# Value tables of a linear-attention kernel: loaded one tile earlier, split in steps, four differences on POOL

## The chip, the cores and the metric

One core of a Trainium2 chip. The metric is the device time of one launch in microseconds, the median of several runs. Times inside a run are microseconds from the start of the profiled span. The engines are PE (TensorE), DVE (VectorE), ACT (ScalarE), POOL (GpSimd) and SP, whose queue issues most transfers.

## The reference

The input x is 2048 tokens by 640 columns. It is normalised and goes into an attention branch and an MLP branch, whose product is added to x. Only the attention's value projection is touched here.

```python
xn = _layernorm(x, axis=-1)
qkv = (xn @ wqkv)                       # 32 heads of 20
pq = einsum("bhsd,hdf->bhsf", q, w_phi) # the same for k
phi = concat([softmax(pq), softmax(-pq)], axis=-1)
kv = einsum("bhsf,bhsd->bhfd", phi_k, v); z = sum_s(phi_k)
o = (phi_q @ kv) / (phi_q @ z + 1e-6)
return x + (o @ wo) * silu(gelu(xn @ w1 + b1) @ w2 + b2)
```

## The kernel before

Tokens are cut into 16 tiles of 128 rows; two tiles make a token pair (`q`). Matmuls work on values split into a high part, rounded to the fp32r format, and a low part, the difference to the original: three passes (high by high, high by low, low by high) make one product. So each weight table is read as a raw fp32 row buffer, copied by ACT into the high part of a slab (`AF.Copy`), and the low part is a subtraction on DVE or POOL.

The first phase runs its code in the order written: every engine carries out its instructions in that order, and a wait holds up all that is behind it on the engine. SP's queue is in that order as well.

*Tiles 6 to 9* (loop `for t in range(6, 10)`): per tile a key projection (`project`, L372), its feature, a value projection and two query projections. `feat1` makes a feature's exponents: three DVE instructions (maximum L384, subtraction L387, minimum L390), one on POOL (L391); `feat2` is ACT's exponential (L400), and `store_e` writes a query's feature to memory through ACT's queue (L695). In the same loop the transposed input of a later token pair is normalised: `pair_sub` on POOL (L341), `pair_mul` on DVE (L346), `pair_plain` rounds it (ACT L285, DVE L287), `t_sums` forms sums of blocks on POOL (L300) and `t_split` rounds those (ACT L321, POOL L323). `pair_stats` stores a pair's mean and deviation (L332) and reads them back spread over the partitions (L334).

*Tiles 10 to 15* (loop `for p in range(5, 8)`): two key projections, then `kv_pair` (L452), which adds the two tiles before to the key-value state and needs POOL's scaled key features (L413), then a value pair. A value pair computes the values of two tiles by a scheme of seven matmul groups (`QPARTS`, L663), which I name X, Y, X2, V, Z, W and S4 in their order. They use sums and differences of weight blocks, made earlier and kept in memory (`sv_dram`, four tables of 128 x 640). Y and V use the first two tables (slabs named `ws`), Z and W the halves that replace part of the direct value weights (`wv`), S4 a slab of two further halves (`ws` again). After X and Y ACT copies the banks to `qx` (L667, L669); V waits for the second copy, X2 for the first. POOL adds the two copies to `qu` (L670), DVE adds V (L674) and then Z (L677), which S4 waits for.

The four tables are loaded at tile 9 (`forms`, L155) and split by `split_to` (L608, L609): the first two after tile 9's last query feature, the `wv` halves between the two key projections of tile 10, the S4 halves inside the value pair, their copies after X and Y (L628), their differences after W (L632), all differences on DVE. The dumps of two query tables (`w_dump`, L208) and the transposed input of pair 7 (`load_xr`, L266, L267) follow the loads on SP.

Row buffers and slabs come from rotating pools; a buffer is taken again when its last reader or its store is done.

Of the kernel before, what the change touches and what calls it, by code (L numbers as in the profile page):

```python
# [8 lines left out]
F32 = mybir.dt.float32  # L9
F32R = mybir.dt.float32r  # L10
AF = mybir.ActivationFunctionType
OP = mybir.AluOpType
# [9 lines left out]
HALF = D // 2  # L22
# [24 lines left out]
def hedgehog_gated_mlp_kernel(ctx: ExitStack, tc: tile.TileContext, x, xt_in, wqk, bd, wv, wo, w1, b1, w2, b2, out_t):  # L47
    nc = tc.nc
# [4 lines left out]
    dram = ctx.enter_context(tc.tile_pool(name="dram", bufs=1, space=bass.MemoryType.DRAM))  # L53
# [27 lines left out]
    def slab(dt, name, shape=(P, 2, D)):  # L81
        return slabs.tile(list(shape), dt, tag="S", name=name)

    def row(shape, dt, name):
        return rows.tile(shape, dt, tag="R", name=name)
# [13 lines left out]
    sv_dram = dram.tile([4, P, D], F32, name="sv_dram")  # L99
# [52 lines left out]
    def load_raw(src, blk=None):  # L152
        raw = row([P, D], F32, "raw")
        dst = raw[:] if blk is None else raw[:].rearrange("p (a b) -> p a b", b=blk)
        nc.sync.dma_start(dst, src)  # L155
        return raw
# [50 lines left out]
    def w_dump(c):  # L207
        nc.sync.dma_start(wq_dram[c], wq_s[c][:, :, :HALF].bitcast(F32))  # L208
# [53 lines left out]
    def load_xr(q):  # L262
        h, p = divmod(q, SLOTS)
        xr = slab(F32, "xr", (P, KC, W2))[:]
        src = xt_in.rearrange("(k p) (h o q t) -> p k h o q t", p=P, h=NH, o=2, q=SLOTS)[:, :, h, :, p]
        nc.sync.dma_start(xr[:, :, :P], src[:, :, 0])  # L266
        nc.sync.dma_start(xr[:, :, P:], src[:, :, 1])  # L267
        xrs[q] = xr
# [25 lines left out]
    def spill(q):  # L294
        nc.sync.dma_start(xp_dram[:, :8, :, at(q)], xp[:, :, :, at(q)].bitcast(F32))
        nc.sync.dma_start(xp_dram[:, 8:, :, at(q)], beside(q).bitcast(F32))
# [47 lines left out]
    def pair_mul(q):  # L344
        bc, xr = pld.pop(q), xrs[q]
        nc.vector.tensor_tensor(xr, xr, bc[:, None, :, 1].to_broadcast([P, KC, W2]), op=OP.mult)  # L346
# [16 lines left out]
    def project(t, ws, mid=None, at_k=3):  # L363
        q, o = divmod(t, 2)
        ps = bankA()
        n = 0
        for k in range(KC):
            if k == at_k and mid is not None:
                mid()
            for a, b in PASSES:  # L370
                for hf in range(2):
                    nc.tensor.matmul(ps[:, hf, :HALF], stat_x(q, o, k, a),  # L372
                                     ws[k][:, b, hf * HALF:(hf + 1) * HALF],
                                     start=n == 0, stop=n == 3 * KC - 1)
                n += 1
        return ps

    def heads(ps):
        return ps[:, :, :HALF].rearrange("p a (h d) -> p a h d", d=DH)

    def feat1(ps, later=None):
        p4 = heads(ps)
        mx = small.tile([P, 2, 16], F32, tag="mx", name="mx")
        nc.vector.tensor_reduce(mx[:], p4, axis=AX.X, op=OP.max)  # L384
        e = slab(F32, "e")[:]
        e5 = e.rearrange("p a (h s d) -> p a h s d", s=2, d=DH)
        nc.vector.tensor_tensor(e5[:, :, :, 0, :], p4, mx[:, :, :, None].to_broadcast([P, 2, 16, DH]),  # L387
                                op=OP.subtract)
        nr = small.tile([P, 2, 16], F32, tag="nr", name="nr")
        last_feat[0] = nc.vector.tensor_reduce(nr[:], e5[:, :, :, 0, :], axis=AX.X, op=OP.min)  # L390
        rest = lambda: nc.gpsimd.tensor_tensor(e5[:, :, :, 1, :], nr[:, :, :, None].to_broadcast([P, 2, 16, DH]),  # L391
                                               e5[:, :, :, 0, :], op=OP.subtract)
        if later is None:
            rest()
        else:
            later.append(rest)
        return e.rearrange("p a b -> p (a b)")

    def feat2(ef):
        nc.scalar.activation(ef, ef, AF.Exp)  # L400
        return ef
# [56 lines left out]
    def kv_pair(t):  # L458
        for u in (t, t + 1):
            kv_acc(u, phis.pop(u), vs.pop(u))  # L460
# [70 lines left out]
    wv_s = []  # L531
# [72 lines left out]
        wq_b.append(sl)  # L604
        nc.sync.dma_start(sl[:, :, :HALF].bitcast(F32), wq_dram[c])

    def split_to(dst, src, eng):
        nc.scalar.activation(dst[:, 0], src, AF.Copy)  # L608
        eng.tensor_tensor(dst[:, 1], src, dst[:, 0].bitcast(F32), op=OP.subtract)  # L609

    def forms(dram, f, base, engs, s4_last=False):
        raws = [load_raw(dram[k]) for k in range(4)]
        yield
        for k in range(4):
            if k < 3:
                f.append(slab(F32R, "ws"))
            if k < 2:
                split_to(f[k][:], raws[k][:], engs[k])
            else:
                split_to(base[k - 2][:, :, HALF:], raws[k][:, HALF:], engs[k])  # L620
            if k == 2 and s4_last:
                continue
            parts = [(f[2][:, :, (j - 2) * HALF:(j - 1) * HALF], raws[j][:, :HALF], engs[j])
                     for j in ((2, 3) if s4_last and k == 3 else (k,) if k >= 2 else ())]
            if s4_last and k == 3:
                yield
            for d, r, _ in parts:
                nc.scalar.activation(d[:, 0], r, AF.Copy)  # L628
            if s4_last and k == 3:
                yield  # L630
            for d, r, eng in parts:
                eng.tensor_tensor(d[:, 1], r, d[:, 0].bitcast(F32), op=OP.subtract)  # L632
            yield

    QPARTS = (("X", "A11", 0, None), ("Y", "S2", 10, None), ("X", "A12", 2, ("A1k", 4)), ("V", "S3", 12, ("A2k", 7)),
# [68 lines left out]
    wq_f, wq_b, wv_f = [], [], []  # L704
# [6 lines left out]
    for t in range(6, 10):  # L711
        q = t - 3
        pk = project(t, wk_s)
        if t == 8:
            kv_pair(6)
            spill(3)
        if t == 9:
            vb = forms(sv_dram, wv_f, wv_s, [nc.vector] * 4, True)
            next(vb)
            w_dump(0)  # L720
            w_dump(1)
        if t == 6:
            next(vf[1])
        es[t] = feat1(pk)
        if t > 6:
            feat2(es[t])
            pair_mul(q)
            pair_plain(q)
            t_sums(q)
        else:  # L730
            pair_sub(4)
            fold_w(wqT, range(4, KC), "wq", wq_s)
            feat2(es[t])
        vs[t] = value(t)
        phis[t] = key_fin(es.pop(t))
        pq = project(next(queries), wq_s)
        ef = feat1(pq)
        if t > 6:
            t_split(q)
            load_xr(q + 1)  # L740
        for u in STATS.get(t, ()):
            pair_stats(u)
        store_e(queries_done.pop(0), ef)
        pq = project(next(queries), wq_s)
        ef = feat1(pq)
        if t == 6:
            next(vf[1])
        if t == 9:
            next(vb)
            next(vb)  # L750
        if t in (7, 8):
            pair_sub(q + 1)
        store_e(queries_done.pop(0), ef)
        if t == 6:
            kv_pair(4)
        for u in XIN.get(t, ()):
            x_in(u)
    qf, later, last_sums = None, [], []
    for p in range(5, 8):
        t = 2 * p  # L760
        pk = project(t, wk_s)
        if p == 7:
            w1r = load_w1(0)
            qf = forms(sq_dram, wq_f, wq_b, [nc.vector, nc.vector, nc.vector, nc.gpsimd])
            next(qf)
        es[t] = feat1(pk)
        if p == 5:
            next(vb)
        if p == 6:
            pair_plain(7)  # L770
        pk = project(t + 1, wk_s)
        kv_pair(t - 2)
        es[t + 1] = feat1(pk, later)
        if p == 7:
            next(qf)
            next(qf)
            q_back(0)
            q_back(1)
            wq_b.extend(wq_s[2:])

        def rest(t=t, p=p):
            if p == 5:
                next(vb)
            later.pop(0)()
            feat2(es[t])
            if p == 6:
                t_sums(7)
            if p == 7:
                next(qf)

        def first_key(t=t, p=p):
            if p == 5:
                next(vb)
            phis[t] = key_fin(es.pop(t))
            feat2(es[t + 1])

        def second_key(t=t, p=p):
            if p < 7:
                phis[t + 1] = key_fin(es.pop(t + 1))
            else:  # L800
                phis[t + 1] = es.pop(t + 1)
                last_sums.append(key_sums(phis[t + 1]))
            if p == 5:
                pair_mul(7)
            if p == 6:
                t_split(7)

        value_pair(p, {1: rest, 2: lambda: p == 7 and next(qf), 3: lambda: p == 5 and pair_sub(7), 4: first_key, 6: second_key})
# [525 lines left out]
```

## Time and profile before

| what | value |
|---|---|
| time, median of 3 runs (657.24 to 657.57) | 657.42 us |
| the profiled execution's own time | 660.41 us |
| its span | 658.7 us |
| mean granted TensorE clock | 0.995 |
| instructions in the span | 11422 |

The profile's page gives each engine's busy time, the slices of the span, and the costliest groups. Other views: the list of waits of one engine (who was waited for, total, times, longest); the timeline (start, duration, engine, line, operation, what it writes and reads, count, and in brackets the idle time before it with its releaser); windows (start and end, length, busy time with count, clock, DMA share, rate).

### The profile page before, as it was taken

To read this page: it belongs to the slowest core of one execution; us is meant where nothing else is said; L and a number is where in the kernel's file an instruction comes from. 1 tells how busy PE (TensorE), PEld (TensorE's weight loads), DVE (VectorE), ACT (ScalarE), POOL (GpSimd) and SP (SyncE) were. 2 spreads that over 40 slices of the span, in tenths; PEclk is the share of its full clock that TensorE was granted. 3 is DMA by queue.
4 is the path that set the end of the run, shared out by engine and by line. 5 is a ranking of instruction groups with operands and counts; after the bars stand their busy time and mean duration, and the time that the engine had idled before them with its cause. 6 is when DMAs were issued, how large, how long until landed. Compare 5 with 4: busy or idle time off the path is not lost.

```text
span 658.7 us, 11422 instructions
## 1 busy us (share of the span) xinstructions
PE 649.6 (99%) x4396; PEld 563.9 (86%) x4396; DVE 488.3 (74%) x739; ACT 237.6 (36%) x345; POOL 396.8 (60%) x366
## 2 busy tenths in 40 slices
PE   9999999999799999999999999999999999999997
PEld 9999999999799998888888888888888886766866
DVE  5785976788976778768979968759789899853232
ACT  3512323324333246252452454751332424132130
POOL 2755477897767864857778876363462967343321
PEclk9999999999799999999999999999999999999999
DMA  9705286466311387537899799596779399999942
GB/s 351 273 1 176 83 295 199 129 212 213 120 42 41 99 270 256 176 102 258 229 256 313 180 410 318 105 331 237 156 215 251 79 266 199 310 244 241 330 162 80
DMA packets 164447, 135.15 MB, mean 205 GB/s; under 512 B 89394, under 2 KB 128562, under 8 KB 164010
## 3 DMA queue, kind: packets, MB, share of 16 engines
q1 hardware_dynamic: 161658, 122.84, 63.7%
q10 hardware_dynamic: 2736, 11.60, 4.5%
q8 instruction: 34, 0.56, 0.4%
q14 instruction: 19, 0.16, 0.1%
HBM read 86.03 MB, written 48.38 MB: 204 GB/s over the span
## 4 chain that ended last, share of the span: by engine, by line
PE 78%; DVE 8%; POOL 6%; DMA 3%; issue 2%; SPq 1%; ACT 1%; ACTq 0%; DVEq 0%; POOLq 0%
PE pB L920 24%; PE pB L891 21%; PE pB L1078 11%; PE pA L372 9%; PE pA L663 6%; PE pB L1025 2%; DMA st_dram<-pst 2%; POOL xr L341 1%; POOL xd L323 1%; POOL e L391 1%; PE qV L663 1%; POOL xr L300 1%; PE pA L174 1%; DVE xr L346 1%; DMA xt<-in_x_dram 1%
## 5 line engine op out<-in xcount | busy, mean ns | idle before, releaser
L920 PE MATMUL pB<-hs,w2s 128*128 128x512 f32 x720 | 165.8, 389 | 0.0
L920 PEld LDWEIGHTS pB<-hs,w2s 128*128 128x128 f32 x720 | 135.0, 188 | 28.8 <-DVE y L929 0.8
L891 PE MATMUL pB<-xp,w1s 128*128 128x512 f32 x324 | 81.4, 389 | 0.2 <-DVE pB L1159 0.2
L891 PE MATMUL pB<-xd,w1s 128*128 128x512 f32 x324 | 79.3, 389 | 0.0
L1078 PE MATMUL pB<-oT,wo 128*128 128x512 f32 (+1 forms) x315 | 72.3, 381 | 0.0
L891 PEld LDWEIGHTS pB<-xp,w1s 128*128 128x128 f32 x324 | 60.7, 188 | 13.2 <-DVE pB L1159 0.7
L891 PEld LDWEIGHTS pB<-xd,w1s 128*128 128x128 f32 x324 | 60.8, 188 | 12.6
L413 POOL TENSOR_TENSOR eq<-eq,rc 128x1280 f32<-128x1280 f32 x16 | 37.9, 2369 | 54.9 <-DVE rc L982 37.7
L1078 PEld LDWEIGHTS pB<-oT,wo 128*128 128x128 f32 x315 | 57.2, 188 | 13.8 <-PE pB L1025 2.5
L929 DVE TENSOR_TENSOR y<-pB,y 128x512 f32<-128x512 f32 x100 | 63.1, 675 | 1.4 <-PE pB L920 1.4
L372 PE MATMUL pA<-wk,xp 128*128 128x320 f32 x384 | 61.7, 317 | 0.0
L896 ACT ACTIVATE pB<-pB,b1t 128x512 f32<-128x512 f32 x48 | 31.8, 662 | 78.8 <-DVE pB L1159 29.2
L400 ACT ACTIVATE e<-e 128x1280 f32<-128x1280 f32 x32 | 40.7, 1273 | 53.2 <-POOL e L391 53.2
L391 POOL TENSOR_TENSOR e<-nr,e 128x640 f32<-128x640 f32 x32 | 43.8, 1368 | 26.1 <-DVE nr L390 23.7
L372 PEld LDWEIGHTS pA<-wk,xp 128*128 128x128 f32 x384 | 59.1, 195 | 0.1
L413 POOL TENSOR_TENSOR e<-e,rc 128x1280 f32<-128x1280 f32 x16 | 38.9, 2433 | 25.4 <-DVE rc L440 25.4
L969 POOL TENSOR_TENSOR ez<-eq,zrep 128x1280 f32<-128x1280 f32 x16 | 47.3, 2959 | 2.5 <-DMA eq<-e_dram 2.5
L480 POOL TENSOR_TENSOR w1s<-raw,w1s 128x640 fp32r<-128x640 f32 (+1 forms) x18 | 25.0, 1388 | 29.9 <-ACT w1s L479 23.8
L372 PE MATMUL pA<-wv,xp 128*128 128x320 f32 x240 | 37.7, 311 | 0.0
L372 PEld LDWEIGHTS pA<-wv,xp 128*128 128x128 f32 x240 | 35.6, 188 | 0.1
L1081 POOL TENSOR_TENSOR xres<-gt,xres 128x256 f32<-128x256 f32 x20 | 14.3, 735 | 35.3 <-DVE gt L1080 35.3
L902 DVE TENSOR_TENSOR hs<-pB,hs 128x512 fp32r<-128x512 f32 x48 | 32.0, 683 | 3.9 <-ACT hs L898 3.6
(184 smaller groups left out, 1143.0 us busy)
## 6 DMA issues: line engine op xcount, KB each, us to landing
raw<-in_w_dram SPq DMA_DIRECT2D x42, 320.0 KB
e_dram<-e ACTq DMA_DIRECT2D x16, 640.0 KB
eq<-e_dram SPq DMA_DIRECT2D x16, 640.0 KB
phi_t<-eq SPq DMA_DIRECT2D x64, 160.0 KB
phT<-phi_t SPq DMA_DIRECT2D x20, 480.0 KB
xt<-in_x_dram SPq DMA_DIRECT2D x16, 320.0 KB
xres<-in_xt_dram SPq DMA_DIRECT2D x20, 256.0 KB
out_dram<-xres SPq DMA_DIRECT2D x18, 256.0 KB
```

The lines of the kernel that those rows point to most:

```text
L372: nc.tensor.matmul(ps[:, hf, :HALF], stat_x(q, o, k, a), ws[k][:, b, hf * HALF:(hf + 1) * HALF], start=n == 0, stop=n == 3 * KC - 1)
L391: rest = lambda: nc.gpsimd.tensor_tensor(e5[:, :, :, 1, :], nr[:, :, :, None].to_broadcast([P, 2, 16, DH]), e5[:, :, :, 0, :], op=OP.subtract)
L400: nc.scalar.activation(ef, ef, AF.Exp)
L413: nc.gpsimd.tensor_tensor(e3, e3, rc[:, :, None].to_broadcast([P, 64, DH]), op=OP.mult)
L663: nc.tensor.matmul(bank[ch], q_x(blk, a, q), p_weight(base, f, w, k)[:, b], start=ch not in seen and n == 0, stop=n == len(mms) - 1, skip_ ...
L891: nc.tensor.matmul(bank[ch][:], tl[:, a, off + wo_:off + wo_ + P], mov(blk, b), start=new and n == 0, stop=n == len(mms) - 1, skip_group_c ...
L896: nc.scalar.activation(ps, ps, AF.Gelu_apprx_tanh, bias=b1t[:, f:f + 1])
L902: nc.vector.tensor_tensor(hs[:, 1], ps, hs[:, 0].bitcast(F32), op=OP.subtract)
L920: nc.tensor.matmul(ps[:], ws[i][:, b, d * P:(d + 1) * P], hs[o][i][:, a, :], start=i == n == 0, stop=(i, n) == (GF - 1, 2), skip_group_che ...
L929: nc.vector.tensor_tensor(y, ps[:], y, op=OP.add)
L969: nc.gpsimd.tensor_tensor(zv, ef, zf, op=OP.mult)
L1078: nc.tensor.matmul(ps[:, mv], w, o[:, mv], start=n == 0, stop=n == 15, skip_group_check=True)
```

## The change

The tables are loaded in tile 8, after the transposed input of pair 6 and ahead of `pair_stats`. A new generator `value_forms` splits them in eight steps, all but the last two within tile 9. Copies (`split_hi`, now L609) and differences (`split_lo`, L613) are separate steps. The first table is copied ahead of tile 9's key feature and its difference stands after it; the second is copied after the pair's `t_split` and its difference stands after the last query feature; the `wv` halves are copied and subtracted right there, the S4 halves after X and Y of the value pair. The differences of the third and fourth table run on POOL. The query tables still use `forms`, in the same order.

```diff
+    def split_hi(parts):
+        for d, r, _ in parts:
+            nc.scalar.activation(d[:, 0], r, AF.Copy)
+
+    def split_lo(parts):
+        for d, r, eng in parts:
+            eng.tensor_tensor(d[:, 1], r, d[:, 0].bitcast(F32), op=OP.subtract)
+
+    def form_parts(raws, f, base, engs, k):
+        if k < 3:
+            f.append(slab(F32R, "ws"))
+        if k < 2:
+            return [(f[k][:], raws[k][:], engs[k])]
+        return [(base[k - 2][:, :, HALF:], raws[k][:, HALF:], engs[k]),
+                (f[2][:, :, (k - 2) * HALF:(k - 1) * HALF], raws[k][:, :HALF], engs[k])]
...
+    def value_forms(raws, engs):
+        parts = []
+        for k in range(2):
+            parts = form_parts(raws, wv_f, None, engs, k)
+            split_hi(parts)
+            yield
+            split_lo(parts)
+            yield
+        parts = [form_parts(raws, wv_f, wv_s, engs, k) for k in (2, 3)]
+        for i in range(2):
+            split_hi([q[i] for q in parts])
+            yield
+            split_lo([q[i] for q in parts])
             yield
...
         if t == 9:
-            vb = forms(sv_dram, wv_f, wv_s, [nc.vector] * 4, True)
+            vb = value_forms(sv_raw, [nc.vector, nc.vector, nc.gpsimd, nc.gpsimd])
             next(vb)
             w_dump(0)
             w_dump(1)
...
         es[t] = feat1(pk)
+        if t == 9:
+            next(vb)
...
             load_xr(q + 1)
+        if t == 8:
+            sv_raw = [load_raw(sv_dram[k]) for k in range(4)]
+        if t == 9:
+            next(vb)
         for u in STATS.get(t, ()):
             pair_stats(u)
...
         if t == 9:
+            next(vb)
             next(vb)
             next(vb)
...
         es[t] = feat1(pk)
-        if p == 5:
-            next(vb)
...
             if p == 5:
                 next(vb)
+                next(vb, None)
             later.pop(0)()
...
-            if p == 5:
-                next(vb)
             phis[t] = key_fin(es.pop(t))
```

How this moves instructions, at three places. First DVE from tile 9's key feature to the key sums of the first value pair. Before, from the last query feature on (`mx`, `e`, `nr` make a feature; `ws` and `wv` are differences of value tables):

```order
L390 TENSOR_REDUCE nr<-e 128x32
L609 TENSOR_TENSOR ws<-raw,ws 128x640 x2
L384 TENSOR_REDUCE mx<-pA 128x32
L387 TENSOR_TENSOR e<-pA,mx 128x32x20
L390 TENSOR_REDUCE nr<-e 128x32
L609 TENSOR_TENSOR wv<-raw,wv 128x320 x2
L384 TENSOR_REDUCE mx<-pA 128x32
L387 TENSOR_TENSOR e<-pA,mx 128x32x20
L390 TENSOR_REDUCE nr<-e 128x32
L674 TENSOR_TENSOR qu<-qu,qV 128x320
L677 TENSOR_TENSOR v<-qu,pA 128x16x20
L632 TENSOR_TENSOR ws<-raw,ws 128x320 x2
```

Six differences stand between the features and behind the sums of the value pair. Now, at the start of tile 9's part, between the key feature and pair 6's multiply and rounding, as a piece of the difference:

```order
 L387 TENSOR_TENSOR e<-pA,mx 128x32x20
 L390 TENSOR_REDUCE nr<-e 128x32
+L613 TENSOR_TENSOR ws<-raw,ws 128x640
 L346 TENSOR_TENSOR xr<-xr,bc 128x1280
 L287 TENSOR_TENSOR xp<-xr,xp 128x5x128
```

One difference moved up to here, one stays after the last query feature, and the other four are gone from DVE. Second, POOL from the last `t_split` of tile 9 into the first value pair, now:

```order
L323 TENSOR_TENSOR xd<-xr,xd 128x4x128
L391 TENSOR_TENSOR e<-nr,e 128x32x20
L613 TENSOR_TENSOR wv<-raw,wv 128x320 x2
L391 TENSOR_TENSOR e<-nr,e 128x32x20
L422 MEMSET v 128x32
L423 MEMSET v 128x32
L682 TENSOR_TENSOR qu<-qx 128x320
L613 TENSOR_TENSOR ws<-raw,ws 128x320 x2
L391 TENSOR_TENSOR e<-nr,e 128x32x20
L341 TENSOR_TENSOR xr<-xr,bc 128x5x128 x2
L413 TENSOR_TENSOR e<-e,rc 128x1280 x2
```

The two rows of L613 are new; the other rows stood there before in the same order (two more memsets left out). Third, ACT from pair 6's sums to the value pair's first copies, now:

```order
L321 ACTIVATE xd<-xr 128x9x128
L609 ACTIVATE ws<-raw 128x640
L400 ACTIVATE e<-e 128x1280
L707 DMA e_dram<-e 128x1280
L609 ACTIVATE wv<-raw 128x320 x2
L400 ACTIVATE e<-e 128x1280
L707 DMA e_dram<-e 128x1280
L679 ACTIVATE qx<-pA 128x320
L681 ACTIVATE qx<-qY 128x320
L609 ACTIVATE ws<-raw 128x320 x2
```

Before, both `ws` copies stood after the first store and the two `wv` copies after the second, right ahead of `qx`; now one `ws` copy stands ahead of the first exponential and the `wv` copies ahead of the second.

More of the change, by code (lines that the diff above doesn't have):

```diff
@@ L605, in q_back, with forms @@
         nc.sync.dma_start(sl[:, :, :HALF].bitcast(F32), wq_dram[c])
[L607 to L611, printed above, removed]
+    def split_hi(parts):
[11 more added lines that the diff above has]
+                (f[2][:, :, (k - 2) * HALF:(k - 1) * HALF], raws[k][:, :HALF], engs[k])]
+    def forms(dram, f, base, engs):
         raws = [load_raw(dram[k]) for k in range(4)]
@@ L614, in forms @@
         for k in range(4):
[L615 to L632, printed above, removed]
+            for part in form_parts(raws, f, base, engs, k):
+                split_hi([part])
+                split_lo([part])
+            yield
[10 more added lines that the diff above has]
+            split_hi([q[i] for q in parts])
+            yield
+            split_lo([q[i] for q in parts])
             yield
```

## The prediction

> **What bounds the kernel now.** I read the busy totals first, then TensorE's own waits, then its timeline around the waits.
>
> ```profile
> PE 649.6 (99%) x4396; PEld 563.9 (86%) x4396; DVE 488.3 (74%) x739; ACT 237.6 (36%) x345; POOL 396.8 (60%) x366
> ...
> PE pA L663 <- ACT qx L667: 1.6, 1, 1.6
> PE pA L663 <- DVE ws L632: 1.4, 2, 1.1
> PE pB L1032 <- DVE y L929: 0.4, 1, 0.4
> ```
>
> TensorE is busy for 99% of the span, so only its holes are to be won. The second view lists who made it wait (total, times, longest). Nearly all of it is on line 663, the token pairs, and the names (qx, ws) are those of the first value pair. TensorE's timeline there, and the same instructions one pair later:
>
> ```profile
> 160.99 1.39 PE L452 MATMUL kv<-e,v 128*32 128x40 f32 x128
> 163.30 1.04 PE L663 MATMUL qY<-ws,xd 128*128 128x320 f32 x6
> 165.94 1.58 PE L663 MATMUL pA<-wv,xp 128*128 128x320 f32 x9 [1.61 <-ACT qx L667]
> 168.68 2.41 PE L663 MATMUL pA<-wv,xd 128*128 128x320 f32 x15
> 171.81 0.42 PE L663 MATMUL pA<-ws,xp 128*128 128x320 f32 x1 [0.72 <-DVE v L677]
> 172.51 0.70 PE L663 MATMUL pA<-ws,xp 128*128 128x320 f32 x3 [0.29 <-DVE ws L632]
> 174.29 0.90 PE L663 MATMUL pA<-ws,xp 128*128 128x320 f32 x2 [1.08 <-DVE ws L632]
> 175.79 6.67 PE L372 MATMUL pA<-wk,xp 128*128 128x320 f32 x30
> 186.79 1.40 PE L452 MATMUL kv<-e,v 128*32 128x40 f32 x128
> ...
> 192.62 2.36 PE L663 MATMUL pA<-wv,xd 128*128 128x320 f32 x15
> 196.14 4.56 PE L372 MATMUL pA<-wk,xp 128*128 128x320 f32 x30
> 205.03 1.38 PE L452 MATMUL kv<-e,v 128*32 128x40 f32 x128
> ```
>
> From one kv group to the next TensorE runs the same work twice: 186.79 - 160.99 = 25.80 us the first time, 205.03 - 186.79 = 18.24 us the second. The first pass is 7.56 us too long, and that is all that any repair of this place can bring. In it are one hole of 1.61 us at X2 (the third group) and three of 0.72 + 0.29 + 1.08 = 2.09 us at S4 (the last). The 30 matmuls that follow take 6.67 us instead of 4.56. The windows of 1 us say why (columns: window, length, TensorE busy, clock, DMA share, GB/s):
>
> ```profile
> 173.00:174.00 1.00, 0.22 (x2) 0.82 0.53 95
> 174.00:175.00 1.00, 0.70 (x3) 0.50 0.59 230
> ...
> 180.00:181.00 1.00, 1.00 (x7) 0.76 0.00 0
> ```
>
> The granted clock falls to half just after the S4 holes and comes back at about 180.2. From 174.29, when matmuls run again, half speed costs 0.36 + 5 x 0.50 + 0.24 = 3.1 us. So the excess of 7.56 is 1.61 + 2.09 of waiting, 3.1 of clock, and 0.8 of refilling after the holes.
>
> **The change part by part.** *The two S4 differences.* Before, they stand on VectorE behind everything else of that pair:
>
> ```profile
> 171.66 2.58 DVE L632 TENSOR_TENSOR ws<-raw,ws 128x320 fp32r<-128x320 f32 x2
> ...
> 212.57 0.87 POOL L632 TENSOR_TENSOR ws<-raw,ws 128x320 fp32r<-128x320 f32 x1
> ```
>
> They end at 174.24 and the last hole ends at 174.29. The change gives them and the two wv differences to POOL, where one costs 0.87 (the same operation in the query tables): 4 x 0.87 = 3.5 us more on POOL. VectorE is rid of the four.
>
> *The first X2 hole.* What ended it is a row of waits on ScalarE, and behind it on POOL:
>
> ```profile
> 158.36 2.84 POOL L323 TENSOR_TENSOR xd<-xr,xd 128x640 fp32r<-128x640 f32 x2
> 160.97 2.73 DVE L609 TENSOR_TENSOR ws<-raw,ws 128x640 fp32r<-128x640 f32 x2 [2.08 <-ACT ws L608]
> 161.16 1.86 POOL L391 TENSOR_TENSOR e<-nr,e 128x640 f32<-128x640 f32 x1
> 163.06 1.27 ACT L400 ACTIVATE e<-e 128x1280 f32<-128x1280 f32 x1 [1.50 <-POOL e L391]
> 164.36 0.33 ACTq L695 DMA_DIRECT2D e_dram<-e  x1
> 165.47 0.42 ACT L667 ACTIVATE qx<-pA 128x320 f32<-128x320 f32 x1
> ```
>
> POOL finishes the last query's feature at 161.16 + 1.86 = 163.02; ScalarE takes its exponential and its store, then two wv copies, then qx, and TensorE goes on. In the change the wv copies stand ahead of that exponential, so from POOL's end to TensorE's restart it is 1.27 + 0.33 + 0.42 and 0.16 of gaps, 2.18 us, instead of 2.92. That is a gain of 0.74. But POOL ends later, as the next two parts make it.
>
> *The first difference, put ahead of pair 6's multiply on VectorE.* VectorE seems to have a gap there:
>
> ```profile
> 143.30 3.15 POOL L341 TENSOR_TENSOR xr<-xr,bc 128x640 f32<-128x640 f32 x2
> 146.41 1.27 POOL L391 TENSOR_TENSOR e<-nr,e 128x640 f32<-128x640 f32 x1
> 146.49 2.55 DVE L346 TENSOR_TENSOR xr<-xr,bc 128x1280 f32<-128x1280 f32 x1 [2.48 <-POOL xr L341]
> 178.86 1.43 DVE L346 TENSOR_TENSOR xr<-xr,bc 128x1280 f32<-128x1280 f32 x1
> 207.59 1.55 DVE L609 TENSOR_TENSOR ws<-raw,ws 128x640 fp32r<-128x640 f32 x2
> ...
> 154.76 0.82 DVE L387 TENSOR_TENSOR e<-pA,mx 128x640 f32<-128x640 f32 x1
> ...
> 144.68 0.33 ACTq L695 DMA_DIRECT2D e_dram<-e  x1
> 160.19 1.37 ACT L608 ACTIVATE ws<-raw 128x640 fp32r<-128x640 f32 x2 [0.48 <-ACT e L400]
> ```
>
> The same multiply takes 2.55 us beside POOL's feature and 1.43 alone: 1.12 us more, about as long as the 1.27 us of POOL that lie over it. So I take it that such instructions of the two engines run one at a time. The upper half for the difference is copied by ScalarE after its store, 145.01 + 0.69 = 145.7, while POOL's subtractions run until 143.30 + 3.15 = 146.45. After 146.45 three must follow each other: the difference 0.78, POOL's feature 1.27, the multiply 1.43. The multiply then ends at 149.93 instead of 146.49 + 2.55 = 149.04, 0.9 us late, and with it pair 6's rounding, its sums and all of POOL up to the last query's feature. The lower bound is nothing, the upper 0.9 + 0.6 if the difference takes the 1.37 that two of them averaged at 160.97.
>
> *The second difference* falls at about 159.8, into POOL's two xd instructions, and by the same reading holds POOL up by 0.78 (bounds 0 and 1.37; before, it held the feature up by 1.86 - 1.27 = 0.59). So POOL's feature ends at 161.20 + 0.9 + 0.78 + 1.27 = 164.1, 1.1 later than before, and TensorE restarts at 164.1 + 2.18 = 166.3 instead of 165.94. The X2 hole grows from 1.6 to about 2.0 us.
>
> *What S4 then waits for.* POOL from 164.1: two wv differences (165.8), a feature (167.1), memsets and qu, as large as a difference (168.3), two S4 differences (170.0). TensorE from 166.3: X2 and V take 168.68 - 165.94 = 2.74, Z and W 15 matmuls of 0.147 (24 in 3.52, from 192.62 to 196.14), so S4 starts at 171.2. POOL is 1.2 us ahead, and VectorE, rid of the 2.73 at 160.97 in that place and of the wv pair, has its sums ready when Z ends: the three S4 holes go, and with them the half clock. If POOL were later than that, S4 would wait again; behind the S4 differences stand the last key's feature and pair 7's subtractions.
>
> *The next wait.* The kv group needs POOL's two scalings:
>
> ```profile
> 179.09 3.42 POOL L413 TENSOR_TENSOR e<-e,rc 128x1280 f32<-128x1280 f32 x1 [0.35 <-DVE rc L440]
> ```
>
> POOL from 170.0: feature 1.27, subtractions 3.15, two scalings of at most 3.42: 181.3. TensorE gets to the kv group at 166.3 + 2.74 + 3.52 + 8.89 (196.14 to 205.03) = 181.4, and needs the second scaling half a group later. It fits, by little.
>
> *The loads and their slots.* The four loads move on SP ahead of pair 7's statistics:
>
> ```profile
> 134.32 0.90 SPq L267 DMA_DIRECT2D xr<-in_xt_dram  x1
> 145.73 3.45 SPq L155 DMA_DIRECT2D raw<-sv_dram  x4
> ...
> 138.00:140.00 2.00, 2.00 (x16) 2.00 (x15) 1.90 (x7) 1.28 (x1) 2.00 (x3) 1.00 0.09 27
> ...
> 89.39 5.67 DMA xt<-in_x_dram
> ```
>
> SP is free from 135.2, so they go out 10 us earlier, into queues that are empty by 138 to 140 (share 0.09). At 5.67 us for a load of this size the first lands by 141, 4 us before ScalarE wants it. The statistics' store waits for POOL anyway; nothing is charged. The slabs are taken earlier too, so two features reuse a buffer whose store went out one store later; the last of them goes out at 144.68 and its buffer is wanted by the feature at 154.76: free, if a store takes under 10 us.
>
> *Sum*, in the profiled execution: the kv group moves from 186.79 to 181.4, 5.4 us. After it, up to the end, TensorE's work and what feeds it follow TensorE, so the end moves by 5.4: span 658.7 to 653.3. The timed median, 657.42, becomes **652.0**. With both differences free of charge POOL ends at 162.5, the restart is at 164.7 and the gain 7.0 (650.4); with both at their longest (165.3, 167.5) the gain is 4.1 (653.3).
>
> **The rivals.** *The half clock stays* (A). The X2 hole is about 2.0 us in one piece; before, 1.61 in one piece left the clock at full, and 2.09 in three pieces within 3.2 us did not. The threshold lies somewhere there. If it trips, the clock price of 3.1 is paid as before: gain 2.3, 655.1. [...]
>
> *The timed runs never had the half clock* (B). The profiled execution took 660.41, 2.99 above the median, close to the 3.1 of the clock. Then only 2.3 can be won there: 655.1. Against it: three runs within 0.33 us, and profiling may cost time of its own.
>
> *The gain is lost later* (C): a stage fed by memory at its own pace takes the 5.4 back, 657.4. Against it: TensorE has no hole above 0.4 us after 186.79.
>
> *The loads are late* (D), the slower side. The copy of the first table stands on ScalarE ahead of the key's exponential, pair 6's rounding and the value copy that TensorE's next projection waits for. If the first load lands x us after 145.0, tile 9 moves by x, a hole of x follows and the half clock with it: x + 3.1 - 5.4. It is slower by more than 0.2% from x = 3.6, a landing 13.4 us after issue; at x = 5 it is 660.1. Against it stand the 5.67 and the empty queues.
>
> **How the numbers follow.** Forecast 0.55 (own range 650.4 to 653.3), A 0.15, B 0.13, C 0.08, D 0.09. A measurement here tells a change from none at about 0.2%, 1.3 us, so faster means below 656.1: the forecast, A and B, 0.83; same 0.08; slower 0.09. The range takes in A and B with the same uncertainty on their side, 650.2 to 655.9, and leaves out C and D.
>
> **What would show it.** In the changed profile: no wait on ws or v at S4; the clock at 1.00 from 165 to 185; qx still the releaser of one hole of 1.5 to 2.5 us; pair 6's multiply ending near 149.9; the kv group near 181.4. A first load landing after 145, a clock of 0.50 anywhere in tile 10, or a hole at the kv group that waits for POOL's scaling would make it wrong.

## The result

| kernel | median | runs | ratio to before, 95% interval |
|---|---|---|---|
| before | 657.24 us | 5 (656.97 to 657.57) | |
| changed | 654.40 us | 5 (653.96 to 654.42) | 0.9955 (0.994 to 0.9969) |

The change makes the kernel 2.84 us faster, about half of the 5.4 forecast. The profiled executions stand 6.00 apart (660.41 and 654.41). The changed kernel's profiled execution agrees with its own median, that of before lies 3 us above its own. Most of what follows is about this difference.

From the changed kernel's page, the busy totals, and TensorE's waits below (us in total, times, longest):

```profile
PE 645.6 (99%) x4396; PEld 560.0 (86%) x4396; DVE 485.5 (74%) x735; ACT 237.6 (36%) x345; POOL 400.3 (61%) x370
```

```profile
PE pA L675 <- ACT qx L679: 1.5, 1, 1.5
PE pB L1048 <- DVE y L945: 0.4, 1, 0.4
```

POOL gained 3.5 us of work, VectorE lost 2.8. The waits on `ws` and `v` are gone; the one on `qx` at X2 is left. TensorE's timeline over the first value pair (start, length, count, idle time before with its releaser):

```profile
160.74 1.39 PE L452 MATMUL kv<-e,v 128*32 128x40 f32 x128
...
165.63 1.58 PE L675 MATMUL pA<-wv,xp 128*128 128x320 f32 x9 [1.54 <-ACT qx L679]
...
170.57 1.04 PE L675 MATMUL pA<-ws,xp 128*128 128x320 f32 x6
...
171.89 4.56 PE L372 MATMUL pA<-wk,xp 128*128 128x320 f32 x30
...
180.78 1.39 PE L452 MATMUL kv<-e,v 128*32 128x40 f32 x128
```

S4 runs its six matmuls in one piece, and the 30 that follow take 4.56 us, the length at full clock (1.00 in every window from 163 to 183 us). From kv to kv it is 20.04 us, against 25.80 in the profiled execution of before and 18.24 in an undisturbed pass. What feeds this place, from the timelines of VectorE, ScalarE and POOL:

```profile
145.73 1.26 DVE L613 TENSOR_TENSOR ws<-raw,ws 128x640 fp32r<-128x640 f32 x1 [1.82 <-ACT ws L609]
146.91 2.56 DVE L346 TENSOR_TENSOR xr<-xr,bc 128x1280 f32<-128x1280 f32 x1
...
144.95 0.74 ACT L609 ACTIVATE ws<-raw 128x640 fp32r<-128x640 f32 x1 [0.46 <-ACT e L400]
...
158.79 3.41 POOL L323 TENSOR_TENSOR xd<-xr,xd 128x640 fp32r<-128x640 f32 x2
162.16 1.27 POOL L391 TENSOR_TENSOR e<-nr,e 128x640 f32<-128x640 f32 x1
...
167.35 1.74 POOL L613 TENSOR_TENSOR ws<-raw,ws 128x320 fp32r<-128x320 f32 x2
...
173.37 5.95 POOL L413 TENSOR_TENSOR e<-e,rc 128x1280 f32<-128x1280 f32 x2
```

The first copy starts at 144.95 without waiting for its load. POOL's last query feature ends at 163.43, its S4 differences at 169.09, 1.48 us ahead of TensorE, its scalings at 179.32, 1.46 ahead of the kv group.

### The profile page after: what moved, and what is told of

It is laid out like the page before. It is cut to its first block, busy times and chain, and to the rows that moved or that the text cites. A ratio compares the mean times of both kernels' runs of the same rounds, so it can differ in the third digit from the quotient of the medians.

```text
span 652.7 us, 11424 instructions
## 1 busy us (share of the span) xinstructions
PE 645.6 (99%) x4396; PEld 560.0 (86%) x4396; DVE 485.5 (74%) x735; ACT 237.6 (36%) x345; POOL 400.3 (61%) x370
## 4 chain that ended last, share of the span: by engine, by line
PE 78%; DVE 8%; POOL 5%; DMA 3%; issue 2%; ACT 2%; SPq 1%; ACTq 0%; DVEq 0%; POOLq 0%
PE pB L936 24%; PE pB L907 21%; PE pB L1094 11%; PE pA L372 9%; PE pA L675 6%; PE pB L1041 2%; POOL e L391 2%; PE qV L675 1%; POOL xr L300 1%; PE pA L174 1%; DVE xr L346 1%; DMA xt<-in_x_dram 1%; PE qY L675 1%; PE kv L452 1%; POOL xr L341 1%
## 5 line engine op out<-in xcount | busy, mean ns | idle before, releaser
L372 PE MATMUL pA<-wk,xp 128*128 128x320 f32 x384 | 59.7, 310 | 0.0
L372 PEld LDWEIGHTS pA<-wk,xp 128*128 128x128 f32 x384 | 56.9, 188 | 0.3 <-ACT v L429 0.2
```

The costliest lines, as they stand in the source:

```text
L372: nc.tensor.matmul(ps[:, hf, :HALF], stat_x(q, o, k, a), ws[k][:, b, hf * HALF:(hf + 1) * HALF], start=n == 0, stop=n == 3 * KC - 1)
```

## The experiments

From the repeats on, every execution comes with its own granted clock, and these clocks became the main evidence. All of them are sorted here by clock (0.998 and above, 0.997 and below); the first five runs of before came without a clock and are left out. An execution at 0.997 or below is counted as one with the half clock: the four profiled executions with so low a mean (0.994 to 0.996) show windows at 0.50, and three profiled ones at a mean of 1.0 (before in its repeat, the differences on VectorE, the changed kernel) show 1.00 in every window from 163 to 182 us. The holes are those of the profiled execution alone, the other executions have no trace. The runs of before were spread over three chips, which agree at full clock (medians 657.06, 657.12 and 657.01), so times of different chips are compared below.

| kernel | holes on TensorE in the profiled execution, from tile 9 to the end of the first value pass, us | clock 0.998 to 1.0: executions, median | 0.994 to 0.997: executions, median |
|---|---|---|---|
| before, all repeats | 1.62; 0.71, 0.30, 1.08 | 34, 657.07 | 43, 658.94 |
| X2 hole filled | 0.64, 0.30, 1.07 | 6, 657.10 | 6, 658.74 |
| changed, both sets | 1.54 (first set); 1.28 (second) | 11, 654.40 | 0 |
| differences on VectorE | 1.51; 0.82 | 8, 656.05 | 1, 656.48 |
| two copies more | 2.41 | 4, 654.98 | 2, 656.59 |
| four copies more | 3.11 | 1, 655.72 | 11, 658.36 |
| POOL alone | 1.38; 0.31, 3.56 | 0 | 5, 660.48 |
| loads late | 5.84 | 0 | 6, 660.72 |
| the four other orders, at the end | 0.33; 0.68; 0.89; none | 24, 652.36 to 654.56 | 0 |

**The kernel before, again** (no edit).

> The kernel before, unchanged, executed again, each execution with its own span and granted clock. Theory 1 (the profiled execution of before held a half clock that its timed runs do not have): most executions take 657.0 to 657.6 us with a span of about 655.5 and a clock of 0.999 or 1.0, and the first value pass from kv to kv takes about 25.80 - 3.1 = 22.7 us. One execution at about 660.4 with a clock of 0.995 may turn up. Theory 2 (every run has the half clock and profiling adds 3 us of its own): the profile shows the span 658.7 and clock 0.995 again, with a kv-to-kv pass of 25.8, while the times stay at 657.2.

657.36 us, ratio 0.9998 (0.9987 to 1.001). This time the profiled execution (657.50, clock 1.0) had the same four holes and no half clock. TensorE's timeline, and the windows in which the clock of the first profile was 0.82 and 0.50 (here 1.00; it stands third from the end, ahead of the DMA share and the GB/s):

```profile
160.59 1.39 PE L452 MATMUL kv<-e,v 128*32 128x40 f32 x128
...
165.83 1.58 PE L663 MATMUL pA<-wv,xp 128*128 128x320 f32 x9 [1.62 <-ACT qx L667]
...
171.68 0.41 PE L663 MATMUL pA<-ws,xp 128*128 128x320 f32 x1 [0.71 <-DVE v L677]
172.39 0.70 PE L663 MATMUL pA<-ws,xp 128*128 128x320 f32 x3 [0.30 <-DVE ws L632]
174.18 0.56 PE L663 MATMUL pA<-ws,xp 128*128 128x320 f32 x2 [1.08 <-DVE ws L632]
...
175.01 4.56 PE L372 MATMUL pA<-wk,xp 128*128 128x320 f32 x30
...
183.90 1.39 PE L452 MATMUL kv<-e,v 128*32 128x40 f32 x128
```

```profile
173.00:174.00 1.00, 0.10 (x1) 0.00 (x0) 1.00 (x1) 0.30 (x1) 1.00 (x2) 1.00 0.50 77
174.00:175.00 1.00, 0.82 (x5) 0.83 (x6) 1.00 (x2) 0.00 (x0) 1.00 (x1) 1.00 0.65 251
```

From kv to kv it is 23.31 us, 0.6 more than the 22.7 expected. So the same program with the same holes runs with or without the half clock. Neither theory is quite right: profiling does not add 3 us (this profiled execution took 0.43 more than the median at full clock, 657.07), as theory 1 says, but the timed runs are not free of the half clock. Each execution draws it or not. The five runs that the changed kernel was first compared with (656.97 to 657.57) all lie within the range of the 34 executions at full clock (656.84 to 657.53) or 0.04 beside it, far from the other group. That all five were at full clock was luck, if each execution draws by itself: at 34 of 77 it happens about once in 60 times. Whether the draws are independent was not tested.

**The four differences back on VectorE**, with early loads and steps kept.

```diff
-            vb = value_forms(sv_raw, [nc.vector, nc.vector, nc.gpsimd, nc.gpsimd])
+            vb = value_forms(sv_raw, [nc.vector] * 4)
```

> The changed kernel with its four differences given back to VectorE; early loads and step by step split stay. Theory 1 (what removed the S4 holes is that the differences stand earlier in program order): S4 still waits for nothing or under 0.3 us, POOL is 3.5 us freer, the wv pair meets POOL's feature at 162 and may lengthen the X2 hole by up to 0.8: 654.4 to 655.4 us. Theory 2 (the move to POOL is what removed them): VectorE is late again, S4 waits 1 us or more and the time goes back to 656 or above.

656.15 us, ratio 0.9973 (0.9963 to 0.9983). TensorE, and VectorE ahead of it:

```profile
171.60 1.15 PE L675 MATMUL pA<-ws,xp 128*128 128x320 f32 x6 [0.82 <-DVE v L689]
...
168.60 1.96 DVE L613 TENSOR_TENSOR ws<-raw,ws 128x320 fp32r<-128x320 f32 x2
170.48 0.47 DVE L686 TENSOR_TENSOR qu<-qu,qV 128x320 f32<-128x320 f32 x1
171.06 0.49 DVE L689 TENSOR_TENSOR v<-qu,pA 128x320 f32<-128x320 f32 x1
```

S4 no longer waits for its weights but for the sum behind them: VectorE does the same work in another order and is late with the last of it. The pass takes 21.41 us (160.51 to 181.92), 1.37 more than in the changed kernel, and the time is 1.75 more. Neither theory came out whole: the wait at S4 (0.82) lies between the 0.3 of theory 1 and the 1 of theory 2, and the time is that of theory 2. Against before at full clock it is still a gain of 1.02 (656.05 against 657.07).

**POOL alone**: the kernel before, four differences on POOL.

```diff
-            vb = forms(sv_dram, wv_f, wv_s, [nc.vector] * 4, True)
+            vb = forms(sv_dram, wv_f, wv_s, [nc.vector, nc.vector, nc.gpsimd, nc.gpsimd], True)
```

> The kernel before with nothing but the engine of four differences changed from VectorE to POOL; loads and order stay as before. Theory 1 (order and early copies are needed): the S4 differences stand on POOL behind its feature and the qu sum, but ScalarE's copies for them are late as before, so part of the 2.09 us of S4 holes stays: 656 to 657 us. Theory 2 (VectorE's load was the whole cause): the S4 holes are gone and the X2 hole stays at about 1.6: 654.4 to 655 us, the whole gain with one edit.

660.48 us against 657.91 for before on the same chip, ratio 1.0046 (1.0034 to 1.0058): slower. Neither expectation had seen what stands ahead of these differences on POOL in the old order, pair 7's subtractions:

```profile
175.03 1.56 PE L663 MATMUL pA<-ws,xp 128*128 128x320 f32 x5 [3.56 <-POOL ws L632]
...
171.09 3.08 POOL L341 TENSOR_TENSOR xr<-xr,bc 128x640 f32<-128x640 f32 x2
174.12 1.68 POOL L632 TENSOR_TENSOR ws<-raw,ws 128x320 fp32r<-128x320 f32 x2
```

One hole of 3.56 us takes the place of three, and the clock falls in all five executions (means of 0.996 and 0.997); against the executions of before at half clock (658.94) the loss is 1.54 us. So POOL is worth something only with the new order, the new order something by itself, and the whole gain needs both.

**Loads at tile 9 again**, with the early copy kept.

```diff
-        if t == 8:
-            sv_raw = [load_raw(sv_dram[k]) for k in range(4)]
...
         if t == 9:
+            sv_raw = [load_raw(sv_dram[k]) for k in range(4)]
             vb = value_forms(sv_raw, [nc.vector, nc.vector, nc.gpsimd, nc.gpsimd])
```

> The changed kernel with its four loads issued at tile 9 as before, while the first copy stays at the head of tile 9. If the loads' place matters, ScalarE waits for the first table: issued at about 135 to 146 on SP (behind the statistics' store that waits for POOL) and landing some 5 us later, at up to 151, against 145.0 where the copy stands: a hole of up to 6 us in the value projection of tile 9, 656 to 661 us. If the loads go out as soon as SP is free (135.2) it makes no difference: 654.4.

660.72 us, ratio 1.0045 (1.0031 to 1.0059). SP issues the loads behind the read-back of the statistics, ScalarE waits for the first, TensorE for ScalarE:

```profile
145.75 0.34 SPq L334 DMA_DIRECT2D bc<-st_dram  x1
146.15 3.96 SPq L155 DMA_DIRECT2D raw<-sv_dram  x4
...
153.12 0.74 ACT L609 ACTIVATE ws<-raw 128x640 fp32r<-128x640 f32 x1 [8.00 <-DMA raw<-sv_dram]
...
158.30 7.17 PE L372 MATMUL pA<-wk,xp 128*128 128x320 f32 x30 [5.84 <-ACT v L429]
```

This is the mechanism of rival D, and the early loads are what keeps it away.

**The last query's exponential behind the first `qx` copy.**

```diff
-        store_e(queries_done.pop(0), ef)
+        if t < 9:
+            store_e(queries_done.pop(0), ef)
...
-        value_pair(p, {1: rest, ...
+        value_pair(p, {0: lambda: p == 5 and store_e(queries_done.pop(0), ef), 1: rest, ...
```

> The changed kernel with the last query's exponential and store moved on ScalarE behind the first qx copy of the value pair. Theory 1 (the 1.54 us hole at X2 is all that is left in this pass, and ScalarE's order alone makes it): the hole is gone, kv to kv goes from 20.04 to about 18.5, the time to about 652.9 us. Rival (POOL is next in line): TensorE then wants S4 at about 169.0 and the second scaling at about 179.2, POOL was done with them at 169.09 and 179.32, so a wait on POOL of up to 1 us comes back: 653.4 to 654 us.

**Pair 6's multiply ahead of the first difference.**

```diff
-        if t == 9:
-            next(vb)
         if t > 6:
             feat2(es[t])
             pair_mul(q)
+            if t == 9:
+                next(vb)
```

> The changed kernel with the first difference put behind pair 6's multiply on VectorE instead of ahead of it. Theory 1 (the difference delays the multiply, and with it POOL's chain up to the last query's feature, as the prediction costed): the multiply ends near 149.0 minus the shift of the trace instead of 149.47, POOL's last feature ends 0.4 to 0.8 us earlier, the X2 hole shrinks from 1.54 to 0.7 to 1.1: 653.6 to 654.0 us. Rival (the delay is hidden, POOL's chain is set elsewhere): no difference, 654.2 to 654.5 us.

653.49 us, ratio 0.9925 (0.9909 to 0.994), and 653.55, ratio 0.9928 (0.991 to 0.9945). In the first kernel the X2 hole is gone, and V waits for the second copy, which now stands behind the exponential. In the second it shrinks:

```profile
165.53 1.14 PE L675 MATMUL qV<-ws,xd 128*128 128x320 f32 x6 [0.33 <-ACT qx L681]
```

```profile
164.62 1.58 PE L675 MATMUL pA<-wv,xp 128*128 128x320 f32 x9 [0.68 <-ACT qx L679]
...
142.72 3.14 POOL L341 TENSOR_TENSOR xr<-xr,bc 128x640 f32<-128x640 f32 x2
...
145.89 2.55 DVE L346 TENSOR_TENSOR xr<-xr,bc 128x1280 f32<-128x1280 f32 x1 [2.42 <-POOL xr L341]
148.36 0.81 DVE L613 TENSOR_TENSOR ws<-raw,ws 128x640 fp32r<-128x640 f32 x1
```

Here the multiply ends 2.58 us after POOL's subtractions (148.44 and 145.86); in the changed kernel it is 3.16 (149.47 and 146.31). The early difference costs that chain 0.58 us. The hole shrank by 0.86, so the rest is not the new order's: in this execution POOL's subtractions, which stand ahead of both instructions, ended 0.45 us earlier (as they did in the first kernel, at 145.87, which keeps the old order there), and TensorE began the pass 0.15 earlier. In the first kernel the time fell into the rival's range, but POOL is not the next in line as the rival had it; TensorE waits for ScalarE. The passes are 18.84 and 19.18.

**Longer holes**: two and four added copies on ScalarE ahead of `qx`, whose result nothing uses. The edit for two:

```diff
         store_e(queries_done.pop(0), ef)
+        if t == 9:
+            idle = const.tile([P, HALF], F32, name="idle")
+            for _ in range(2):
+                nc.scalar.activation(idle[:], wq_s[2][:, 0, :HALF].bitcast(F32), AF.Copy)
```

> The changed kernel with two added copies of 320 elements on ScalarE ahead of qx (0.42 us each); their result is used nowhere. The X2 hole grows from 1.54 to about 2.4. Theory 1 (the clock is halved by how much of a stretch of some us is idle, here 2.4 in one piece against 1.62 + 2.09 within 9 us before): no half clock in most executions, 655.2 us, clock 0.999. Theory 2 (a hole of more than about 2 us is enough): clock 0.995 to 0.997 and 656.7 to 658 us in many.

> The same with four such copies: the X2 hole grows to about 3.2 us. Theory 1: the threshold lies between 3.2 and the 3.56 us that halved the clock in every execution of the kernel with POOL alone, so most executions stay at 0.999, 656.1 us. Theory 2 (2 us is enough): 0.995 to 0.997 in nearly all, 657.6 to 659 us.

655.06 us, ratio 0.9954 (0.9936 to 0.9971), and 658.16, ratio 0.9993 (0.998 to 1.0006). The kernels with profiled holes of 2.41 and 3.11 us have the half clock in 2 of 6 and in 11 of 12 executions. Theory 1 holds for the first and fails for the second; theory 2 the other way round. In the kernels with one long hole these counts show no sharp threshold in its length, but a share of executions that grows with it: 0 of 11 with 1.54 and 1.28 us, 2 of 6 with 2.41, 11 of 12 with 3.11, 5 of 5 with 3.56 (POOL alone, behind 1.38 and 0.31), 6 of 6 with 5.84 (late loads). In the kernel with four copies, one of its long draws:

```profile
167.38 2.77 PE L675 MATMUL pA<-wv,xp 128*128 128x320 f32 x9 [3.11 <-ACT qx L679]
```

```profile
166.00:167.00 1.00, 0.00 (x0) 0.00 (x0) 0.10 (x1) 0.94 (x3) 0.45 (x5) 0.84 0.99 415
167.00:168.00 1.00, 0.62 (x2) 0.62 (x3) 0.00 (x0) 1.00 (x5) 0.27 (x1) 0.50 0.01 0
...
173.00:174.00 1.00, 1.00 (x7) 1.00 (x6) 0.18 (x2) 0.00 (x0) 1.00 (x2) 0.75 0.19 74
```

**X2 hole filled, S4 holes kept**: in the kernel before, group Y of the first value pair is run three times.

```diff
-            for n, (w, k, b, blk, a) in enumerate(mms):
-                nc.tensor.matmul(
+            for _ in range(3 if i == 1 and q == 5 and out else 1):
+                for n, (w, k, b, blk, a) in enumerate(mms):
+                    nc.tensor.matmul(
```

> The kernel before with the second group (Y) of its first value pair run three times instead of once, with the same result: 12 matmuls, about 1.8 us of TensorE work, lie in the X2 hole, and the three S4 holes of 2.09 us stay. Theory 1 (the hole at X2 and the holes at S4 add up in what trips the clock): with the first of them filled nearly all executions stay at 0.998 or more, 657.0 to 657.3 us. Theory 2 (the S4 holes alone trip it): the clock falls in about half of the executions as before (28 of 50 so far), 658.5 to 659 us in these.

657.89 us, ratio 1.0002 (0.999 to 1.0015), half clock in 6 of 12. Theory 2: the S4 holes alone bring it. The X2 hole is filled:

```profile
162.91 2.80 PE L664 MATMUL qY<-ws,xd 128*128 128x320 f32 x18
165.54 1.48 PE L664 MATMUL pA<-wv,xp 128*128 128x320 f32 x9
```

**The changed kernel again.**

> The changed kernel again, beside runs of the kernel before on one chip. Theory 1 (each execution of the kernel before draws the half clock or not, the changed kernel does not): the changed kernel stays at 654.0 to 654.5 us with a clock of 0.999 or 1.0 in all its executions, while before falls into two groups, about 657.1 at 0.998 or more and about 658.8 at 0.997 or less; against the first group the gain is 2.7, against the second 4.4. Rival (the changed kernel has the half clock now and then too): one or more of its executions at 0.997 and about 655.5 to 656.

654.40 us (654.22 to 654.80), ratio 0.9947 (0.9932 to 0.9961) against 657.51 for before, whose 16 executions fell 8 to 8. Theory 1, except that two executions (654.65 and 654.80) lie above its 654.5. Against the executions of all repeats at full clock the gain is 657.07 - 654.40 = 2.67, against the others 658.94 - 654.40 = 4.54.

**Both orders together**, with the exponential behind the S4 copies.

```diff
                 next(vb)
                 next(vb, None)
+                store_e(queries_done.pop(0), ef)
```

> Both orders of the two runs before put together: pair 6's multiply ahead of the first difference, and the last query's exponential and store behind both qx copies and the S4 copies. No hole at X2, no wait of V on qx: kv to kv near 18.5 and 652.9 to 653.2 us, against 653.49 and 653.55 with one of them. Rival (POOL is next): its S4 differences wait for ScalarE's copies or the second scaling is late, and TensorE waits up to 0.5: 653.4 to 653.9 us.

654.10 us (653.89 to 654.30), ratio 0.9942 (0.9929 to 0.9956): worse than either alone. Two exponentials in a row now stand ahead of the copy that frees bank X:

```profile
165.19 1.26 ACT L400 ACTIVATE e<-e 128x1280 f32<-128x1280 f32 x1
166.48 0.33 ACTq L707 DMA_DIRECT2D e_dram<-e  x1
166.86 1.27 ACT L400 ACTIVATE e<-e 128x1280 f32<-128x1280 f32 x1 [0.40 <-POOL qu L682]
168.04 0.42 ACT L684 ACTIVATE v<-pA 128x320 f32<-128x320 f32 x1
...
168.51 1.58 PE L675 MATMUL pA<-wv,xd 128*128 128x320 f32 x9 [0.89 <-ACT v L684]
```

**The exponential behind that copy too.**

```diff
-                store_e(queries_done.pop(0), ef)
...
-        ... 2: lambda: p == 7 and next(qf), ...
+        ... 2: lambda: (p == 7 and next(qf), p == 5 and store_e(queries_done.pop(0), ef)), ...
```

> As the run with both orders, but with the last query's exponential and store behind the copy of the value row as well, the copy that TensorE's W group waited 0.89 us for. Theory 1 (that copy's place on ScalarE is the last thing in this pass that costs anything): no hole between the two kv groups, kv to kv about 18.4 us, 652.7 to 653.1 us. Rival (the pass is clean but something behind it, a reuse of the later stored feature's buffer or a memory-fed stage, takes it back): kv to kv about 18.4 and still 653.4 us or more.

652.69 us (652.36 to 653.11), ratio 0.9919 (0.9905 to 0.9934), all six executions at 0.998 or above: the best version, 1.71 below the changed kernel's 654.40 (measured on another chip). The pass has no hole and takes 178.91 - 160.67 = 18.24 us, the undisturbed length:

```profile
160.67 1.39 PE L452 MATMUL kv<-e,v 128*32 128x40 f32 x128
...
178.91 1.39 PE L452 MATMUL kv<-e,v 128*32 128x40 f32 x128
```

## Why the prediction was right in its mechanism and wrong in its size

**The step that failed** is the last of the sum: "the end moves by 5.4 ... The timed median, 657.42, becomes 652.0". The 5.4 contain 3.1 us of half clock, worked out from one execution that had drawn it, and were taken off a median of three that had not, by their times. Rival B said this at a chance of 0.13, and the repeats showed it, though not quite as B had it: timed runs have the half clock too, in 43 of 77 executions, only not in these. It was to be had from the numbers of before: the profiled execution lay 2.99 us above the median, as much as the clock term. "Profiling may cost time of its own" was the wrong way out; in the repeat the profiled execution took 657.50, that of the changed kernel 654.41 with a median of 654.40.

**The sum without that term.** B's gain was 2.3. The X2 hole came out at 1.54 instead of 2.0, which adds 0.46: 2.8, and 2.84 was measured. That the two meet is in part luck. In the two profiles at full clock the pass became 23.31 - 20.04 = 3.27 us shorter, since the four holes of before cost 23.31 - 18.24 - 3.71 = 1.36 beyond their length, not 0.8, and the one that is left 0.26; the medians at full clock are 2.67 apart. The 3.1 was too dear for this pass as well: with and without the half clock it took 25.80 and 23.31, 2.49 apart. And the clock did not fall just after the S4 holes, as the prediction read it, but within the last of them, at about 173.64.

**S4's holes go**: right. For all of them to go, the step-by-step split and POOL are both needed: with POOL alone the hole is 3.56 us, with the steps alone there is one of 0.82, of another cause.

**The half clock goes with them**: right, 0 of 11 executions against 43 of 77.

**The early difference.** Predicted 0.9 us on POOL's chain, measured 0.58: it started at 145.73, while POOL was still at its subtractions (until 146.31), and took 1.26 instead of 0.78, so 0.58 us of it ran beside them, where the prediction had it begin behind them. The second difference was priced at 0.78; POOL's xd pair took 3.41 against 2.84 before, 0.57. Together they are 0.5 too dear, and with a start of the pass 0.25 earlier than in the first profile POOL's feature ended at 163.43, not 164.1.

**POOL's slack.** 1.2 us predicted at S4 and about nothing at the kv group; 1.48 and 1.46 measured. The two scalings took 5.95 together, where 3.42 each had been allowed.

**The loads** were in time. D's formula charged a late landing in full: a landing 8.1 us late (153.12 against 145.0) would have made 657.42 + 8.1 + 3.1 - 5.4 = 663.2, and 660.72 was measured. ScalarE had over 2 us of slack there, so the hole was 5.84, and the pass behind it lost its X2 hole as well, having gained time.

**A** rested on a threshold that a single hole of 2.0 us might pass. No run shows a threshold: with a profiled hole of 2.41 the clock fell in 2 of 6 executions, with 1.54 and 1.28 in none of 11.

**C** did not happen: the kv group moved by 6.01 us between the two profiled executions and the end of the span by 6.0.

## What to carry to other kernels

Before a price is taken from a profiled execution, hold its own time against the timed median: where they differ by as much as one term, that term may be one that only some executions pay, and it must be summed against executions of the same kind. When work is moved to an emptier engine, list what stands ahead of it there in program order; the same move was worth 1.4 us in the value pass with the new order, and cost 1.5 us (660.48 against 658.94, both at half clock) with the old. When an instruction is put off to end one wait, find every copy that it now stands ahead of: with the multiply first, the last exponential gave 653.55 us ahead of `qx`, 654.10 behind the S4 copies and 652.69 behind the value copy.

## What the runs showed of the hardware

**The half clock lasted 3.42 us in one trace and 6.82 to 6.84 in three.** Its ends can be placed from the clock of the windows in which it begins and ends: 0.82 means that 0.18 / 0.5 = 0.36 us of that microsecond ran at 0.50. In the first profile of before it went from 173.64 to 180.48, 6.84 us; with four copies from 166.68 to 173.50, 6.82. With POOL alone, and with late loads:

```profile
176.00:177.00 1.00, 1.00 (x5) 1.00 (x6) 0.00 (x0) 0.00 (x0) 1.00 (x1) 0.54 0.82 236
...
179.00:180.00 1.00, 1.00 (x7) 1.00 (x7) 0.96 (x3) 0.00 (x0) 0.00 (x0) 0.75 0.72 195
```

```profile
157.00:158.00 1.00, 0.00 (x0) 0.00 (x0) 1.00 (x2) 1.00 (x3) 0.06 (x1) 0.52 1.02 306
...
163.00:164.00 1.00, 1.00 (x6) 1.00 (x6) 1.00 (x2) 0.57 (x1) 1.00 (x1) 0.57 0.00 0
```

These are 176.08 to 179.50, 3.42 us, and 157.04 to 163.86, 6.82 us, twice as long. By the author's estimate, 3.42 us of work at 0.50 cost 3.42 x 0.50 = 1.7 us, and 6.82 us cost 3.4. Read so, it fits the times of before, of which only the first profile has a trace with the half clock: 657.07 at full clock, 40 executions from 657.81 to 659.35, three from 660.03 to 660.55 (the first profile's 660.41 would be one of these). The prediction's 3.1 was thus also near the dearer of these two prices.

What brings the half clock about was not shown. The longest holes in the four traces that have it are 1.61 us (before), 3.11 (four copies), 3.56 (POOL alone) and 5.84 (late loads). In the 3.42 us up to the fall of the clock TensorE was idle for about 1.4 us in before, 2.4 with POOL alone and with four copies, and all the time with late loads. Yet before stayed at 1.00 in the profile of its repeat, with nearly the same holes (1.62; 0.71, 0.30, 1.08), and the changed kernel, with 1.54 us in one piece in its first profile, had a mean clock of 0.999 or 1.0 in all 11 executions. So idle time as the profile shows it does not decide alone, and why before has the half clock in 43 of 77 executions stays open.

**A hole cost more than its length.** Over the undisturbed 18.24 us the passes with one hole of 0.33, 0.68, 0.89 and 1.54 us take 0.60, 0.94, 1.14 and 1.80 more: 0.25 to 0.27 us on top of each. With several holes it is more for each: 0.84 for the two of the kernel with the differences on VectorE (21.41 - 18.24 - 2.33), and 1.36 for the four of before, where the prediction had 0.8 and called it refilling. What it consists of was not tested.
